# A reordered prologue, rows turned by DMA, and a weight load moved by three steps, in a fused attention and gated-MLP kernel

## The chip, the cores and the metric

One core of a Trainium2 chip. The metric is device time in microseconds (us) of one execution. "Start" below is the time from the beginning of the profile to the first exponential of the attention. A "half" is one head with 1024 of the 2048 queries: 16 steps of one key block each. The half-rate state of TensorE is read below from the distance between the starts of consecutive matmuls: 0.216 us for 512 columns and 0.056 us for 128 at full rate, 0.427 and 0.107 us at half rate (the "cold array" of some passages).

## The reference

A block with adaptive layer norm. Shapes: x is 2048 x 1024, 32 heads of 128 with cached keys and values of 2048 rows, an MLP of 2 x 1792 columns, everything bf16.

```python
mod = (_silu(c) @ w_mod).reshape(c.shape[0], 6, 1, -1)        # sa, ca, ga, sb, cb, gb
h = _layernorm(x, axis=-1) * (1 + ca) + sa
x = x + ga * _A_ref(h, A_k_cache, A_v_cache, A_wq, A_wo)       # q = h @ wq, softmax(q k / sqrt(128)) v, @ wo
h = _layernorm(x, axis=-1) * (1 + cb) + sb
x = x + gb * _B_ref(h, B_w_in, B_w_sp, B_b_sp, B_w_out)        # gelu, layer norm, spatial gate, projection
```

## The kernel before

It runs in stages: a prologue (norm of the first eight row tiles, modulation of h1T, first query product), attention over 64 halves, the output projection with the second norm, then the MLP. Three places matter.

The prologue alternates row loads and modulation-weight loads, and takes head 0's keys through a transposing DMA:

```python
    load_wm(nc.scalar, 0, 1)
    load_wm(nc.scalar, 1, 1)
    for j in range(4):
        for t in range(2):
            nc.sync.dma_start(xg[j][:, t], x_dram[:, 2 * j + t, :])
        load_wm(nc.sync, j, 0)
    ...
    load_wq(0)
    load_kv(0)          # keys with transpose=True
    load_wq(1)
    for fn in q_work(0, 0, bank_ps):
        fn()
    emit_s(0)
    emit_s(1)
```

In attention the loads for the next head, and every fourth head a 1 MB load of query weights, are issued at step 2 of a half. The softmax sums of the half before go through DRAM and a transposing DMA, issued at step 3 in the same queue; VectorE reduces them at step 10:

```python
        if kb == 2 and i < 16:
            load_kv(halves[i + 1][0])
            if i == 12:
                load_wq(2)
        elif kb == 2 and qh == 0 and h + 1 < H:
            load_kv(h + 1)
            if h % 4 == 2 and h + 2 < H:
                load_wq((h + 2) // 4)
        ...
                    {0: store_sums, 3: turn_sums, 10: finish_den, 13: load_rec}).get(kb)
```

In the output projection, each of 16 row tiles is turned into columns on TensorE, one tile behind:

```python
    def to_columns(h, hT, ti):
        hps = bank_ps("hps", [P, KD, P], BF16)
        for dc in range(KD):
            nc.tensor.transpose(hps[:, dc, :], h[:, dc * P:(dc + 1) * P], identity[:])
        nc.vector.tensor_copy(out=hT[:, :, ti * P:(ti + 1) * P], in_=hps[:, :, :])
    ...
    for ti in range(NT):
        ...
        attend_out(ti, range(H) if ti else [H - 1])          # 64 matmuls of 512 columns
        if ti > 0:
            to_columns(hbs.pop(ti - 1), h2T, ti - 1)
```

The softmax here doesn't subtract the row's maximum and nothing guards it: scores larger than these inputs give would overflow.

Of the kernel before, what the change touches and what calls it, by code (L numbers as in the profile page):

```python
# [16 lines left out]
def kernel(  # L17
# [62 lines left out]
    h1_dram = dram.tile([2, P, D], BF16)  # L80
    mod_dram = dram.tile([4, D], FP32)
    rec_dram = dram.tile([2 * H, 1024], FP32)

# [17 lines left out]
    for j in range(4):  # L101
        xg.append(early.tile([P, 2, D], BF16, name=f"xg{j}"))
        wms.append(early.tile([P, 2, KD, 256], BF16, name=f"wm{j}"))

    def load_wm(eng, j, k):
        eng.dma_start(wms[j][:, k], wmod_v[:, :, k * D + j * 256:k * D + (j + 1) * 256])

    load_wm(nc.scalar, 0, 1)
    load_wm(nc.scalar, 1, 1)
    for j in range(4):  # L110
        for t in range(2):
            nc.sync.dma_start(xg[j][:, t], x_dram[:, 2 * j + t, :])
        load_wm(nc.sync, j, 0)

# [24 lines left out]

    def to_columns(h, hT, ti):  # L140
        hps = bank_ps("hps", [P, KD, P], BF16)
        for dc in range(KD):
            nc.tensor.transpose(hps[:, dc, :], h[:, dc * P:(dc + 1) * P], identity[:])  # L143
        nc.vector.tensor_copy(out=hT[:, :, ti * P:(ti + 1) * P], in_=hps[:, :, :])  # L144

    h1T = ring.tile([P, KD, S], BF16, name="h1T")
# [7 lines left out]
    def silu():  # L154
        nc.tensor.transpose(cT_ps[:], c_sb[:, :], identity[:KD, :KD])
        nc.scalar.activation(e_sb[:], cT_ps[:], ACT.Exp, scale=-1.0)
        load_wm(nc.scalar, 2, 1)
        load_wm(nc.scalar, 3, 1)

# [8 lines left out]
    def keep_busy(n):  # L168
        zps = bank_ps("zps", [P, 512])
        for _ in range(n):  # L170
            nc.tensor.matmul(zps[:], zeros[:, 0:P], zeros[:], start=True, stop=True)
# [3 lines left out]
    def mod_products(j):  # L175
        mps = mpss[j] = side_ps("mps", [P, 2, 2])
        for k in range(2):
            for f in range(2):
                for kc in range(KD):
                    nc.tensor.matmul(mps[:, k, f:f + 1], wms[j][:, k, kc, f * P:(f + 1) * P],  # L180
                                     scT[:, kc:kc + 1], start=(kc == 0), stop=(kc == KD - 1))
# [6 lines left out]

    def modulate(dc, t0, eng=nc.vector):
        sl = h1T[:, dc, t0:t0 + 1024]  # L190
        if eng is nc.scalar:
            nc.scalar.activation(sl, sl, ACT.Identity, bias=cols[:, 0, dc:dc + 1],
                                 scale=cols[:, 1, dc:dc + 1])
            return
        nc.vector.tensor_scalar(out=sl, in0=sl, scalar1=cols[:, 1, dc:dc + 1],
                                scalar2=cols[:, 0, dc:dc + 1], op0=ALU.mult, op1=ALU.add)

    row = {}
    silu()
    for ti in range(9):  # L200
        if ti < 8:
            row[ti] = row_stats(xg[ti // 2][:, ti % 2, :])
        if ti == 0:
            silu_end()
        else:
            xt = xg[(ti - 1) // 2][:, (ti - 1) % 2, :]
            centre(xt, row.pop(ti - 1), xt)
            if ti % 2 == 0:
                j = ti // 2 - 1
                hps = wide_ps("hps", [P, 2, KD, P], BF16)  # L210
                for t in range(2):
                    for dc in range(KD):
                        nc.tensor.transpose(hps[:, t, dc, :],
                                            xg[j][:, t, dc * P:(dc + 1) * P], identity[:])
                nc.scalar.activation(
                    h1T[:, :, j * 256:(j + 1) * 256].rearrange("p d (t k) -> p d t k", t=2),
                    hps[:].rearrange("p t d k -> p d t k"), ACT.Copy)
                if j > 0:
                    mod_products(j - 1)
                keep_busy(6)  # L220
            elif ti > 3:
                mod_columns(ti // 2 - 2)
    mod_products(3)
    mod_columns(2)
    for j in range(4):
        if j == 3:
            mod_columns(3)
        modulate(2 * j, 0)
        modulate(2 * j + 1, 0, nc.scalar if j else nc.vector)
    keep_busy(8)  # L230

    wq_v = A_wq.rearrange("(dc p) hd -> p dc hd", p=P)
    wo_v = A_wo.rearrange("(h p) n -> p h n", p=P)
    wq_g = {}
    kts, vs, qts = {}, {}, {}

# [50 lines left out]

    load_wq(0)
    load_kv(0)
    load_wq(1)  # L290
    for fn in q_work(0, 0, bank_ps):
        fn()
    emit_s(0)
    emit_s(1)
# [57 lines left out]

    accs, slabs, hbs = {}, {}, {}

# [23 lines left out]
    def late_rows(g):  # L378
# [3 lines left out]
        if 4 <= g < 100:  # L382
            if r == 0:
                rows[ti] += row_stats(rows[ti][0][:, :]),
                if ti + 1 < NT:
                    load_row(ti + 1)
            elif r == 2:
                xt, st = rows.pop(ti)
                hb = early.tile([P, D], BF16, name="hb1", tag="hb1", bufs=2)
                centre(xt[:, :], st, hb[:])  # L390
                nc.sync.dma_start(h1_dram[ti % 2], hb[:])
            elif r == 6:
                nc.sync.dma_start(out=h1T[:, :, ti * P:(ti + 1) * P], in_=h1_dram[ti % 2],
                                  transpose=True)
        elif 100 <= g < 108:
            modulate(g - 100, 1024)

# [7 lines left out]
    def late_mods(i, kb):  # L405
        n0, odd = divmod(i - 17, 2)
        if n0 < 8 and not odd and kb == 2:
            wm_l[n0] = early.tile([P, KD, 512], BF16, name="wm_l", tag="wm_l", bufs=2)
            nc.sync.dma_start(wm_l[n0][:], wmod_v[:, :, (n0 + 4) * 512:(n0 + 5) * 512])
# [15 lines left out]
        elif i == 33 and kb == 8:  # L425
            wide_rows = early.tile([P, 2, D], FP32, name="wide_rows")
            nc.sync.dma_start(ga[:], mod_dram[0].partition_broadcast(P))
# [5 lines left out]
    for g, (i, kb) in enumerate(steps):  # L433
# [13 lines left out]
        if kb == 2 and i < 16:  # L447
            load_kv(halves[i + 1][0])
            if i == 12:
                load_wq(2)  # L450
        elif kb == 2 and qh == 0 and h + 1 < H:
            load_kv(h + 1)
            if h % 4 == 2 and h + 2 < H:
                load_wq((h + 2) // 4)
        if i == len(halves) - 1 and kb == 7:
# [58 lines left out]
    def load_x(ti):  # L514
        xts[ti] = mid.tile([P, D], BF16, name="x_in", tag="x_in", bufs=3)
        nc.sync.dma_start(xts[ti][:], x_dram[:, ti, :])

    load_x(0)
    load_x(1)
# [4 lines left out]
    for ti in range(NT):  # L524
# [8 lines left out]
        if ti > 0:  # L533
            to_columns(hbs.pop(ti - 1), h2T, ti - 1)
        x1 = mid.tile([P, D], BF16, name="x1", tag="x1", bufs=2)
# [7 lines left out]
        ln_mod(x1[:, :], mod2, hb)  # L543
        hbs[ti] = hb
    right.__exit__(None, None, None)
# [5 lines left out]
    for ti in range(NT):  # L551
        zst = small.tile([P, 4, nc.vector.BN_STATS_DIM], FP32, name="zst", tag="zst")
        for k in range(4):
# [6 lines left out]
            nc.vector.bn_stats(out=zst[:, k, :], in_=z2[ti][:, sl])  # L560
            if ti == 2 and k == 0:
                to_columns(hbs.pop(NT - 1), h2T, NT - 1)
        mv, rstd = ln_stats(zst[:, :, :])
# [114 lines left out]
```

## Time and profile before

Median 1877.88 us over 12 runs (1875.40 to 1880.30).

| read from the trace of before | us |
|---|---|
| start (first exponential) | 34.29 |
| start to the first projection matmul | 1124.61 |
| projection, to the first matmul of the next stage | 227.95 |
| next stage (second MLP half) | 97.43 |
| rest | 391.47 |

The page's first part: busy us of each engine, share of the span, instructions.

```profile
span 1875.7 us, 24842 instructions
PE 1847.7 (99%) x9129; PEld 853.1 (45%) x9129; DVE 1271.8 (68%) x2124; ACT 1099.9 (59%) x1155; POOL 32.7 (2%) x55
```

TensorE is the bound, but its 99% says little about what a piece of its work costs. The Trainium skill, "Perfetto Trace Analysis" (Identifying the Most-Contended Engine), warns that the busy share of matmuls is no good measure of how close a kernel is to its peak, because matmuls are pipelined.

The timeline of TensorE in the projection: start, duration of the merged group, line, output and inputs, count.

```profile
1200.60 0.59 PE L372 MATMUL acc<-wo_t,oT_last 128*128 128x512 bf16 x2
1201.03 0.61 PE L143 MATMUL hps<-identity,hb 128*128 128x128 bf16 x8
1201.47 13.54 PE L372 MATMUL acc<-wo_t,ot 128*128 128x512 bf16 x62
1214.86 0.59 PE L372 MATMUL acc<-wo_t,oT_last 128*128 128x512 bf16 x2
```

A row tile takes 1214.86 - 1200.60 = 14.26 us. The eight transposes are shown as 0.61 us long, but the next group starts 1201.47 - 1201.03 = 0.44 us after them: the durations of pipelined groups overlap.

The waits of VectorE in attention (waiting group, releaser: total us, times, longest):

```profile
DVE den L325 <- DMA pT<-sums_dram: 14.1, 7, 2.9
```

One of these waits, in a half that loads query weights, in two timelines of before: first that of the issuing queue (SPq), then that of VectorE:

```profile
534.26 2.06 SPq L244 DMA_TRANSPOSE kT<-in_A_k_cache_dram  x1
536.41 0.53 SPq L246 DMA_DIRECT2D v_sb<-in_A_v_cache_dram  x1
537.00 1.55 SPq L239 DMA_DIRECT2D wq_t<-in_A_wq_dram  x1
538.60 2.97 SPq L318 DMA_TRANSPOSE pT<-sums_dram  x1
```

```profile
544.04 0.09 DVE L323 MEMSET rec<- 128x32 f32 x1
547.04 1.22 DVE L325 TENSOR_REDUCE den<-pT 128x8 f32<-128x1024 bf16 x1 [2.92 <-DMA pT<-sums_dram]
```

The sums are issued behind the weights, and VectorE, which has casts of the next queries behind this reduction, stands for 2.92 us. TensorE then loses 1.71 us at 550 us. Six such TensorE gaps add up to 6.7 us (distances between the starts of consecutive matmuls in the trace, less the 0.22 us that a matmul takes: 0.95, 0.86, 1.71, 0.73, 1.21, 1.26).

The start of before, on ScalarE: the last line is the first exponential.

```profile
26.97 3.50 ACT L192 ACTIVATE h1T<-h1T,cols 128x1024 bf16<-128x1024 bf16 x3
34.29 2.85 ACT L458 ACTIVATE pt<-sps 128x1024 bf16<-128x1024 f32 x3 [3.82 <-PE sps L282]
```

### The profile page before, as it was taken

What the parts mean: (1) busy time and instruction counts of PE and PEld (TensorE: products, weight loads), DVE (VectorE), ACT (ScalarE), POOL (GpSimd) and SP (SyncE); (2) the same over time, 40 slices, a digit from 0 to 9 for tenths busy, and PEclk for the clock granted to TensorE, in tenths of its full rate; (3) what the DMA queues carried; (4) which work ended last, traced back from release to release, by engine and by line L of the source; (5) the groups of instructions that cost most, each with busy time, mean ns of one, the idle gap of its engine ahead of it and who ended that gap; (6) DMA issues with size and microseconds to landing.
All of it is one profiled execution on the core that took longest, in us unless ns stands there. A gap on an engine that the chain in (4) does not pass through costs nothing.

```text
span 1875.7 us, 24842 instructions
## 1 busy us (share of the span) xinstructions
PE 1847.7 (99%) x9129; PEld 853.1 (45%) x9129; DVE 1271.8 (68%) x2124; ACT 1099.9 (59%) x1155; POOL 32.7 (2%) x55
## 2 busy tenths in 40 slices
PE   7999999999999999999999999999999999999999
PEld 4444444444444444444444444444445444444444
DVE  6898888888888888888888887554465400333334
ACT  5888999988988999989989997000013332000000
POOL 1000000000000000000000000000000000000000
PEclk9999999999999999999999999999999999999999
DMA  9575576465565644565466334664123012221102
GB/s 241 119 169 115 130 162 149 122 158 139 126 163 127 151 129 110 131 165 138 126 164 144 105 91 122 182 199 122 45 65 76 12 46 79 51 52 45 45 1 79
DMA packets 387963, 215.30 MB, mean 115 GB/s; under 512 B 289536, under 2 KB 345856, under 8 KB 387840
## 3 DMA queue, kind: packets, MB, share of 16 engines
q1 hardware_dynamic: 383680, 211.62, 44.3%
q10 hardware_dynamic: 4160, 2.10, 0.4%
q8 instruction: 71, 1.16, 0.3%
q14 instruction: 52, 0.43, 0.1%
HBM read 126.36 MB, written 41.44 MB: 89 GB/s over the span
## 4 chain that ended last, share of the span: by engine, by line
PE 90%; DVE 4%; DMA 4%; issue 1%; SPq 1%; ACT 0%; POOL 0%; DVEq 0%; POOLq 0%
PE sps L282 21%; PE ops L469 20%; PE acc L372 12%; PE gps L607 10%; PE qps L262 10%; PE zps L557 5%; PE bo L628 5%; PE zps L591 5%; DMA pT<-sums_dram 3%; DVE pacc L479 2%; DMA xg<-in_A_x_dram 1%; SPq L239 0%; DVE stats L127 0%; DMA wm<-in_w_mod_dram 0%; DVE den L325 0%
## 5 line engine op out<-in xcount | busy, mean ns | idle before, releaser
L458 ACT ACTIVATE pt<-sps 128x1024 bf16<-128x1024 f32 x1024 | 1017.7, 1025 | 110.2 <-PE sps L282 77.6
L479 DVE TENSOR_TENSOR pacc<-pacc,pt 128x1024 bf16<-128x1024 bf16 x896 | 616.6, 688 | 64.1 <-ACT pt L458 4.7
L282 PE MATMUL sps<-qT,kT 128*128 128x512 bf16 x2048 | 610.0, 379 | 7.0 <-DVE qT L266 6.3
L469 PE MATMUL ops<-pt,v_sb 128*128 128x512 bf16 x2048 | 609.4, 379 | 1.5 <-DVE ou L475 1.2
L262 PE MATMUL qps<-h1T,wq_t 128*128 128x512 bf16 x1024 | 344.4, 379 | 1.5 <-DVE rec L337 1.2
L469 PEld LDWEIGHTS <-v_sb 128*128 128x128 bf16 x2048 | 200.1, 98 | 249.2 <-issue 8.5
L282 PEld LDWEIGHTS <-kT 128*128 128x128 bf16 x2048 | 199.0, 98 | 245.4 <-issue 10.1
L372 PE MATMUL acc<-wo_t,ot 128*128 128x512 bf16 x992 | 216.9, 379 | 0.0
L559 ACT ACTIVATE z<-zps 128x448 bf16<-128x448 f32 x64 | 34.8, 543 | 290.3 <-PE zps L557 287.4
L607 PE MATMUL gps<-wsp,z 128*128 128x512 bf16 x896 | 193.9, 379 | 0.0
L610 DVE TENSOR_TENSOR g<-gps,b_bc 128x512 bf16<-128x512 f32 x56 | 38.7, 692 | 221.8 <-PE gps L607 221.8
L262 PEld LDWEIGHTS <-wq_t 128*128 128x128 bf16 x1024 | 100.2, 98 | 120.8
L372 PEld LDWEIGHTS <-ot 128*128 128x128 bf16 x992 | 96.4, 98 | 113.5
L607 PEld LDWEIGHTS <-z 128*128 128x128 bf16 x896 | 87.7, 98 | 105.7
L266 DVE CAST qT<-qps 128x512 bf16<-128x512 f32 x128 | 88.4, 690 | 42.7 <-PE qps L262 42.6
L557 PE MATMUL zps<-z2w,h2T 128*128 128x448 bf16 x512 | 97.3, 352 | 0.0
L628 PE MATMUL bo<-w_out_t,z1T 128*128 128x512 bf16 x448 | 97.2, 379 | 0.0
L591 PE MATMUL zps<-h2T,z1w 128*128 128x512 bf16 x448 | 96.9, 379 | 0.0
L144 DVE COPY h2T<-hps 128x1024 bf16<-128x1024 bf16 x16 | 11.0, 690 | 97.4 <-PE hps L143 97.4
L346 DVE TENSOR_TENSOR oT<-ou,rbc 128x1024 bf16<-128x1024 f32 x62 | 75.6, 1219 | 1.0 <-DMA rbc<-rec_dram 1.0
L325 DVE TENSOR_REDUCE den<-pT 128x8 f32<-128x1024 bf16 x55 | 65.3, 1188 | 14.1 <-DMA pT<-sums_dram 14.1
L557 PEld LDWEIGHTS <-h2T 128*128 128x128 bf16 x512 | 50.0, 98 | 46.5 <-issue 0.2
(72 smaller groups left out, 689.1 us busy)
## 6 DMA issues: line engine op xcount, KB each, us to landing
rbc<-rec_dram SPq DMA_DIRECT2D x64, 512.0 KB
v_sb<-in_A_v_cache_dram SPq DMA_DIRECT2D x40, 512.0 KB
oT_dram<-oT SPq DMA_DIRECT2D x62, 256.0 KB
sums_dram<-pacc SPq DMA_DIRECT2D x55, 256.0 KB
ot<-oT_dram SPq DMA_DIRECT2D x24, 512.0 KB
wq_t<-in_A_wq_dram SPq DMA_DIRECT2D x8, 1024.0 KB
wm_l<-in_w_mod_dram SPq DMA_DIRECT2D x8, 1024.0 KB
wo_t<-in_A_wo_dram SPq DMA_DIRECT2D x8, 1024.0 KB
```

Source lines behind the costliest of these rows:

```text
L262: nc.tensor.matmul(box["ps"][:], wq_t[:, dc, hc:hc + DH], h1T[:, dc, q0:q0 + 512], start=(dc == 0), stop=(dc == KD - 1))
L266: nc.vector.tensor_copy(out=out_t[:, j * 512:(j + 1) * 512], in_=box["ps"][:])
L282: nc.tensor.matmul(sps[:, j * 512:(j + 1) * 512], kts[h][:, kb * P:(kb + 1) * P], qts[(h, qh)][:, j * 512:(j + 1) * 512], start=True, stop ...
L346: nc.vector.tensor_mul(out=oT[:], in0=state[i]["ou"][:], in1=state[i]["rbc"][:])
L372: nc.tensor.matmul(accs[ti][:, sl], lhs, wo_t[:, hh, sl], start=(hh == 0), stop=(hh == H - 1))
L458: nc.scalar.activation(pt[:], s_tiles.pop(g)[:], ACT.Exp, scale=SCALE)
L469: nc.tensor.matmul(o_ps[j][:], vs[h][:, kb, :], pt[:, j * 512:(j + 1) * 512], start=(kb == 0), stop=(kb == NKB - 1))
L479: nc.vector.tensor_add(out=pacc[:], in0=pacc[:], in1=pt[:])
L557: nc.tensor.matmul(zps[:], h2T[:, dc, ti * P:(ti + 1) * P], z2w[:, dc, sl], start=(dc == 0), stop=(dc == KD - 1))
L591: nc.tensor.matmul(zps[:], w[:, dc, :], h2T[:, dc, q * 512:(q + 1) * 512], start=(dc == 0), stop=(dc == KD - 1))
L607: nc.tensor.matmul(gps[:], z2[s][:, f * P:(f + 1) * P], wsps[q][:, s, :], start=(s == 0), stop=(s == NT - 1))
L628: nc.tensor.matmul(bo[:], z1T[:, f, ti * P:(ti + 1) * P], w_out_t[:, f, sl], start=(f == 0), stop=(f == NF - 1))
```

## The change

Its intent is to start attention earlier, and to take work and stalls off TensorE:

1. Prologue: row tiles first; statistics of two tiles on ScalarE; head 0's keys loaded plainly and turned on TensorE; the last turned tile modulated straight out of PSUM by both ScalarE and VectorE; 13 instead of 32 dummy matmuls.
2. The query-weight load moves from step 2 to step 5 of a half.
3. Rows of the output projection are stored to DRAM and come back through a transposing DMA.

```diff
+    h2_dram = dram.tile([4, P, D], BF16)
 ...
-    for j in range(4):
-        for t in range(2):
-            nc.sync.dma_start(xg[j][:, t], x_dram[:, 2 * j + t, :])
-        load_wm(nc.sync, j, 0)
+    for ti in range(8):
+        nc.sync.dma_start(xg[ti // 2][:, ti % 2], x_dram[:, ti, :])
+    load_wm(nc.sync, 0, 0)
+    load_wm(nc.sync, 2, 1)
+    ...                                   # (1, 0), (3, 1), (2, 0), (3, 0)
+    nc.sync.dma_start(wq_g[0][:, :, 0:256], wq_v[:, :, 0:256])
+    nc.sync.dma_start(k0[:], A_k_cache[0, 0].rearrange("(p j) d -> p j d", p=P))
+    nc.sync.dma_start(vs[0][:], A_v_cache[0, 0].rearrange("(p j) d -> p j d", p=P))
+    nc.sync.dma_start(wq_g[0][:, :, 256:512], wq_v[:, :, 256:512])
 ...
+    turn(1)
+    mod_columns(0)
+    mod_products(1)
+    keep_busy(4)
+    ...
+    turn(2)
+    mod_columns(1)
+    mod_products(2)
+    norm(6)
+    norm(7)
+    turn(3, False)
+    keep_busy(5)
+    mod_products(3)
+    mod_columns(2)
+    for dc in range(4):
+        modulate(dc, 0, 768)
+    mod_columns(3)
+    modulate(7, 0, 768, nc.scalar)
+    for dc in (4, 5):
+        modulate(dc, 0, 768)
+        modulate(dc, 768, 256, nc.scalar, turned_x[3][:, dc, :, :])
+    modulate(6, 0, 768)
+    for dc in range(4):
+        modulate(dc, 768, 256, nc.vector, turned_x[3][:, dc, :, :])
+    for dc in (6, 7):
+        modulate(dc, 768, 256, nc.scalar, turned_x[3][:, dc, :, :])
 ...
-            if i == 12:
-                load_wq(2)
         elif kb == 2 and qh == 0 and h + 1 < H:
             load_kv(h + 1)
-            if h % 4 == 2 and h + 2 < H:
-                load_wq((h + 2) // 4)
+        if kb == 5 and i == 12:
+            load_wq(2)
+        elif kb == 5 and i >= 16 and qh == 0 and h % 4 == 2 and h + 2 < H:
+            load_wq((h + 2) // 4)
 ...
+    def turn_rows(ti):
+        nc.sync.dma_start(out=h2T[:, :, ti * P:(ti + 1) * P], in_=h2_dram[ti % 4],
+                          transpose=True)
 ...
-            to_columns(hbs.pop(ti - 1), h2T, ti - 1)
+            turn_rows(ti - 1)
 ...
-        hbs[ti] = hb
+        nc.sync.dma_start(h2_dram[ti % 4], hb[:])
```

More of the change, by code (lines that the diff above doesn't have):

```diff
@@ L102 @@
         xg.append(early.tile([P, 2, D], BF16, name=f"xg{j}"))
-        wms.append(early.tile([P, 2, KD, 256], BF16, name=f"wm{j}"))
+        wms.append(early.tile([P, 2, KD, 256], BF16, name="wm", tag="wm", bufs=4))
     def load_wm(eng, j, k):
         eng.dma_start(wms[j][:, k], wmod_v[:, :, k * D + j * 256:k * D + (j + 1) * 256])
+    k0 = early.tile([P, NKB, DH], BF16, name="k0")
+    wq_v = A_wq.rearrange("(dc p) hd -> p dc hd", p=P)
+    wq_g, kts, vs, qts = {}, {}, {}, {}
+    for g in range(2):
+        wq_g[g] = att.tile([P, KD, 4 * DH], BF16, name="wq_t", tag="wq_t", bufs=2)
+    kts[0] = att.tile([P, S], BF16, name="kT", tag="kT", bufs=2)
+    vs[0] = att.tile([P, NKB, DH], BF16, name="v_sb", tag="v_sb", bufs=2)
+    nc.scalar.activation(small.tile([P, 1], FP32, name="warm_e")[:], eps_tile[:], ACT.Exp)
     load_wm(nc.scalar, 0, 1)
     load_wm(nc.scalar, 1, 1)
-    for j in range(4):
-        for t in range(2):
-            nc.sync.dma_start(xg[j][:, t], x_dram[:, 2 * j + t, :])
-        load_wm(nc.sync, j, 0)
+    for ti in range(8):
+        nc.sync.dma_start(xg[ti // 2][:, ti % 2], x_dram[:, ti, :])
+    load_wm(nc.sync, 0, 0)
+    load_wm(nc.sync, 2, 1)
+    load_wm(nc.sync, 1, 0)
+    load_wm(nc.sync, 3, 1)
+    load_wm(nc.sync, 2, 0)
+    load_wm(nc.sync, 3, 0)
+    nc.sync.dma_start(wq_g[0][:, :, 0:256], wq_v[:, :, 0:256])
+    nc.sync.dma_start(k0[:], A_k_cache[0, 0].rearrange("(p j) d -> p j d", p=P))
+    nc.sync.dma_start(vs[0][:], A_v_cache[0, 0].rearrange("(p j) d -> p j d", p=P))
+    nc.sync.dma_start(wq_g[0][:, :, 256:512], wq_v[:, :, 256:512])
     def ln_stats(chunks):
@@ L138, in ln_mod @@
         nc.vector.tensor_add(out=h[:], in0=h[:], in1=mod[:, 1, :])
-    def to_columns(h, hT, ti):
-        hps = bank_ps("hps", [P, KD, P], BF16)
-        for dc in range(KD):
-            nc.tensor.transpose(hps[:, dc, :], h[:, dc * P:(dc + 1) * P], identity[:])
-        nc.vector.tensor_copy(out=hT[:, :, ti * P:(ti + 1) * P], in_=hps[:, :, :])
     h1T = ring.tile([P, KD, S], BF16, name="h1T")
@@ L156, in silu @@
         nc.scalar.activation(e_sb[:], cT_ps[:], ACT.Exp, scale=-1.0)
-        load_wm(nc.scalar, 2, 1)
-        load_wm(nc.scalar, 3, 1)
     def silu_end():
@@ L168, in keep_busy @@
     def keep_busy(n):
-        zps = bank_ps("zps", [P, 512])
+        zps = side_ps("zps", [P, 512])
         for _ in range(n):
@@ L175, in mod_products @@
     def mod_products(j):
-        mps = mpss[j] = side_ps("mps", [P, 2, 2])
+        mps = mpss[j] = bank_ps("mps", [P, 2, 2])
         for k in range(2):
@@ L187, in mod_columns, with modulate @@
                                     scalar1=1.0)
-    def modulate(dc, t0, eng=nc.vector):
-        sl = h1T[:, dc, t0:t0 + 1024]
+    def modulate(dc, t0, n, eng=nc.vector, src=None):
+        dst = h1T[:, dc, t0:t0 + n]
+        if src is None:
+            src = dst
+        else:
+            dst = dst.rearrange("p (t k) -> p t k", k=P)
         if eng is nc.scalar:
-            nc.scalar.activation(sl, sl, ACT.Identity, bias=cols[:, 0, dc:dc + 1],
+            nc.scalar.activation(dst, src, ACT.Identity, bias=cols[:, 0, dc:dc + 1],
@@ L193, in modulate @@
                                  scale=cols[:, 1, dc:dc + 1])
             return
-        nc.vector.tensor_scalar(out=sl, in0=sl, scalar1=cols[:, 1, dc:dc + 1],
+        nc.vector.tensor_scalar(out=dst, in0=src, scalar1=cols[:, 1, dc:dc + 1],
                                 scalar2=cols[:, 0, dc:dc + 1], op0=ALU.mult, op1=ALU.add)
-    row = {}
-    silu()
-    for ti in range(9):
-        if ti < 8:
-            row[ti] = row_stats(xg[ti // 2][:, ti % 2, :])
-        if ti == 0:
-            silu_end()
-        else:
-            xt = xg[(ti - 1) // 2][:, (ti - 1) % 2, :]
-            centre(xt, row.pop(ti - 1), xt)
-            if ti % 2 == 0:
-                j = ti // 2 - 1
-                hps = wide_ps("hps", [P, 2, KD, P], BF16)
-                for t in range(2):
-                    for dc in range(KD):
-                        nc.tensor.transpose(hps[:, t, dc, :],
-                                            xg[j][:, t, dc * P:(dc + 1) * P], identity[:])
-                nc.scalar.activation(
-                    h1T[:, :, j * 256:(j + 1) * 256].rearrange("p d (t k) -> p d t k", t=2),
-                    hps[:].rearrange("p t d k -> p d t k"), ACT.Copy)
-                if j > 0:
-                    mod_products(j - 1)
-                keep_busy(6)
-            elif ti > 3:
-                mod_columns(ti // 2 - 2)
@@ new lines, with stats_act, norm @@
+    row, junk = {}, early.tile([P, D], BF16, name="junk")
+    def stats_act(ti):
+        mv = early.tile([P, 2], FP32, name=f"mv{ti}")
+        src = xg[ti // 2][:, ti % 2, :]
+        nc.scalar.activation(junk[:], src, ACT.Identity, scale=1.0 / D, accum_out=mv[:, 0:1])
+        nc.scalar.activation(junk[:], src, ACT.Square, scale=D ** -0.5, accum_out=mv[:, 1:2])
+        row[ti] = (mv, None)
+    def norm(ti):
+        mv, rstd = row.pop(ti)
+        x_t = xg[ti // 2][:, ti % 2, :]
+        centre(x_t, (mv, rstd), x_t)
@@ new lines, in finish_act @@
+    def finish_act(ti):
+        mv = row[ti][0]
+        var = small.tile([P, 1], FP32, name="var", tag="var")
+        nc.vector.scalar_tensor_tensor(out=var[:], in0=mv[:, 0:1], scalar=mv[:, 0:1],
+                                       in1=mv[:, 1:2], op0=ALU.mult, op1=ALU.subtract)
+        nc.vector.tensor_scalar(out=var[:], in0=var[:], scalar1=-1.0, scalar2=EPS,
+                                op0=ALU.mult, op1=ALU.add)
+        rstd = small.tile([P, 1], FP32, name="rstd", tag="rstd")
+        nc.gpsimd.tensor_tensor(out=rstd[:], in0=var[:], in1=neg_half[:], op=ALU.pow)
+        row[ti] = (mv, rstd)
@@ new lines, with turn, dve @@
+    turned_x = {}
+    def turn(j, evacuate=True):
+        hps = turned_x[j] = wide_ps("hps", [P, KD, 2, P], BF16)
+        for t in range(2):
+            for dc in range(KD):
+                nc.tensor.transpose(hps[:, dc, t, :],
+                                    xg[j][:, t, dc * P:(dc + 1) * P], identity[:])
+        if evacuate:
+            nc.scalar.activation(
+                h1T[:, :, j * 256:(j + 1) * 256],
+                hps[:].rearrange("p d t k -> p d (t k)"), ACT.Copy)
+    def dve(ti):
+        row[ti] = row_stats(xg[ti // 2][:, ti % 2, :])
@@ new lines, in turn_k, with out @@
+    def turn_k(j, evacuate=True):
+        k_ps = bank_ps("k_ps", [P, 8, DH], BF16)
+        for kb in range(8):
+            nc.tensor.transpose(k_ps[:, kb, :], k0[:, 8 * j + kb, :], identity[:])
+        def out():
+            nc.scalar.activation(kts[0][:, 1024 * j:1024 * (j + 1)],
+                                 k_ps[:].rearrange("p j d -> p (j d)"), ACT.Copy)
+        if evacuate:
+            out()
+        return out
+    silu()
+    dve(0)
+    silu_end()
+    dve(1)
+    norm(0)
+    stats_act(2)
@@ L223 @@
+    dve(3)
+    norm(1)
+    turn(0)
+    keep_busy(4)
+    mod_products(0)
+    finish_act(2)
+    stats_act(5)
+    dve(4)
+    norm(2)
+    norm(3)
+    turn(1)
+    mod_columns(0)
+    mod_products(1)
+    keep_busy(4)
+    dve(6)
+    norm(4)
+    finish_act(5)
+    dve(7)
+    norm(5)
+    turn(2)
[5 more added lines that the diff above has]
+    keep_busy(5)
     mod_products(3)
     mod_columns(2)
-    for j in range(4):
-        if j == 3:
-            mod_columns(3)
-        modulate(2 * j, 0)
-        modulate(2 * j + 1, 0, nc.scalar if j else nc.vector)
@@ L230 @@
-    keep_busy(8)
-    wq_v = A_wq.rearrange("(dc p) hd -> p dc hd", p=P)
+    for dc in range(4):
[10 more added lines that the diff above has]
+        modulate(dc, 768, 256, nc.scalar, turned_x[3][:, dc, :, :])
@@ L233 @@
     wo_v = A_wo.rearrange("(h p) n -> p h n", p=P)
-    wq_g = {}
-    kts, vs, qts = {}, {}, {}
     def load_wq(g):
@@ L286, in emit_s @@
         s_tiles[g] = sps
-    load_wq(0)
-    load_kv(0)
-    load_wq(1)
-    for fn in q_work(0, 0, bank_ps):
-        fn()
+    nc.sync.dma_start(wq_g[1][:], wq_v[:, :, 512:1024])
+    first = q_work(0, 0, bank_ps)
+    for fn in first[:KD]:
+        fn()
+    turn_k(0)
+    for fn in first[KD:]:
+        fn()
+    turn_k(1)
     emit_s(0)
@@ L351, in normalise @@
         del state[i]
-    accs, slabs, hbs = {}, {}, {}
+    accs, slabs = {}, {}
     def load_slab(s, pl):
@@ L395, in late_rows @@
         elif 100 <= g < 108:
-            modulate(g - 100, 1024)
+            modulate(g - 100, 1024, 1024)
     def load_row(ti):
@@ L407, in late_mods @@
         if n0 < 8 and not odd and kb == 2:
-            wm_l[n0] = early.tile([P, KD, 512], BF16, name="wm_l", tag="wm_l", bufs=2)
+            wm_l[n0] = early.tile([P, KD, 512], BF16, name="wm_l", tag="wm", bufs=4)
             nc.sync.dma_start(wm_l[n0][:], wmod_v[:, :, (n0 + 4) * 512:(n0 + 5) * 512])
@@ L425, in late_mods @@
         elif i == 33 and kb == 8:
-            wide_rows = early.tile([P, 2, D], FP32, name="wide_rows")
+            wide_rows = early.tile([P, 2, D], FP32, name="wide_rows", tag="wm", bufs=4)
             nc.sync.dma_start(ga[:], mod_dram[0].partition_broadcast(P))
@@ L543 @@
         ln_mod(x1[:, :], mod2, hb)
-        hbs[ti] = hb
+        nc.sync.dma_start(h2_dram[ti % 4], hb[:])
+    turn_rows(NT - 1)
     right.__exit__(None, None, None)
@@ L560 @@
             nc.vector.bn_stats(out=zst[:, k, :], in_=z2[ti][:, sl])
-            if ti == 2 and k == 0:
-                to_columns(hbs.pop(NT - 1), h2T, NT - 1)
         mv, rstd = ln_stats(zst[:, :, :])
```

## The prediction

> **What bounds the kernel now.** TensorE. The page's busy table gives PE 99% of a 1875.7 us span, VectorE 68%, ScalarE 59%; clock 1.00. In the timeline most halves of a head (80 matmuls of 512 columns at 0.216 us) take 17.3 us, and a row tile of the output projection 14.26 us: 64 x 0.213 = 13.65 plus 0.61 for eight transposes. So only TensorE work, TensorE stalls and the prologue count. The first exponential starts at 34.29 us.
>
> **The change, part by part.**
>
> 1. Output projection: 128 TensorE transposes and 16 VectorE copies become a store plus a transposing DMA per row tile. Eight transposes occupy TensorE 0.61 us (timeline): 16 x 0.61 = 9.8 us, all critical, since the stage has no TensorE gap. The copies (11.0 us) are off the path. The added traffic (two transfers of 256 KB per 13.65 us) fits: the stage runs at about 150 GB/s (1250 to 1300 us), against 320 in the prologue. The last transpose is needed only at the end of the next stage, some 85 us later. Expected: -9.8 us; tile period 13.65 us.
>
> 2. The 1 MB query-weight load moves from step 2 of a half to step 5, so behind the transposing load of the softmax sums issued at step 3. By the waits, VectorE's denominator reduction waits for that load 14.1 us over 7 times, longest 2.9. Six TensorE gaps of 0.73 to 1.71 us (at 266, 407, 550, 691, 831, 970 us) sit in the six halves that load weights: 6.7 us. Expected: -6 us; those waits almost gone.
>
> 3. Prologue: row tiles are loaded before most modulation weights, two tiles' statistics go to ScalarE, head 0's keys are turned on TensorE instead of by DMA. The DMAs run at 315 to 325 GB/s from 4 to 24 us, so rows plus modulation weights (6.3 MB) cannot land before about 22 us in any order. VectorE needs about 15 us from the first row (estimate: six statistics of 1.55, eight normalisations of 0.54, small ones), so ends about 20 us: DMA limits. Then: last modulation products 0.94 us, modulations to 25-26, first query product (weights land about 24), key transposes, second query product to 28, casts, and a ScalarE key copy of about 1 us just ahead of the first exponential. Estimate: first exponential at 30.0 us, -4.3 us. There are 13 instead of 32 dummy matmuls. The Trainium skill, "TensorE: Matmul & The Clock Gate" (Part 1), says the array starts at half rate and speeds up after about 3.4 us of activity; this trace agrees (dummy matmuls 0.43 us apart until about 16 us, later 0.22). Gaps could cool it again and cost 1-2 us.
>
> The rest of attention, gating and final projection are unchanged; the early halves limited by VectorE (gaps of about 4 us between 70 and 161 us) stay.
>
> **Predicted time.** 1878.2 - 9.8 - 6.0 - 4.3 = 1858 us, 80% range 1853 to 1863. Faster by over 2%: 0.01; within 2%: 0.98; slower by over 2%: 0.01.
>
> **Right if** the first exponential starts at 28.5-31.5 us; the six gaps are gone; the projection period is 13.65 us; later stages are unchanged, less one 0.61 us transpose group. **Wrong if** TensorE waits for projection slabs or transposed rows; new waits for weights or reciprocals appear; matmuls are 0.43 us apart between 20 and 34 us.
>
> **What would make it wrong.** Transposing DMAs slowing the slab loads, which share their queue; a cold array at the start of attention; weights or keys of head 0 landing after 26 us; VectorE debt from the prologue in the early halves.

## The result, and the profile after

Median 1861.10 us over 8 runs (1859.89 to 1862.49). The ratio of the mean of its runs to that of before's runs of the same rounds is 0.9912, 95% interval 0.9902 to 0.9922 (so not quite the ratio of the medians). Executions over 1.5% slower than the fastest of the same kernel are left out of the means. The saving is 1877.88 - 1861.10 = 16.8 us where 19.9 had been predicted: inside the range, within 2%, but with terms that were off in both directions. By stage, from the two traces (one execution each, so their sum, 16.0 us, is not the difference of the medians):

| stage | before | after | change | predicted |
|---|---|---|---|---|
| start | 34.29 | 32.62 | -1.67 | -4.3 |
| start to first projection matmul | 1124.61 | 1117.65 | -6.96 | -6.0 |
| projection | 227.95 | 221.25 | -6.70 | -9.2 |
| next stage | 97.43 | 96.85 | -0.58 | -0.6 |
| rest | 391.47 | 391.35 | -0.12 | 0 |

(The predicted 9.8 is split over two stages, 15 and 1 groups of 0.61.)

The page's first part and TensorE's timeline in the projection, after:

```profile
span 1859.7 us, 24646 instructions
PE 1837.9 (99%) x8998; PEld 845.0 (45%) x8998; DVE 1262.1 (68%) x2110; ACT 1102.8 (59%) x1167; POOL 32.8 (2%) x55
```

```profile
1191.51 0.59 PE L451 MATMUL acc<-wo_t,oT_last 128*128 128x512 bf16 x2
1191.94 13.54 PE L451 MATMUL acc<-wo_t,ot 128*128 128x512 bf16 x62
1205.33 0.59 PE L451 MATMUL acc<-wo_t,oT_last 128*128 128x512 bf16 x2
```

A row tile takes 1205.33 - 1191.51 = 13.82 us, not the predicted 13.65, and TensorE never waits in this stage.

The wait of the reduction for the sums is absent from the list of waits. The queue in a half that loads weights:

```profile
530.29 2.15 SPq L320 DMA_TRANSPOSE kT<-in_A_k_cache_dram  x1
532.54 0.53 SPq L322 DMA_DIRECT2D v_sb<-in_A_v_cache_dram  x1
533.12 2.98 SPq L397 DMA_TRANSPOSE pT<-sums_dram  x1
536.16 0.57 SPq L427 DMA_DIRECT2D oT_dram<-oT  x1
536.77 0.43 SPq L315 DMA_DIRECT2D wq_t<-in_A_wq_dram  x1
```

The sums stand ahead of the weights now. Of the TensorE gaps over 0.3 us between 200 and 1140 us, one of 0.63 us is left, at 635 us; it is none of the six (before has one of 0.50 us at 641 us besides them).

The start in the timelines of after, first on ScalarE, then on VectorE (in brackets: idle before, and what ended it):

```profile
26.40 1.03 ACT L205 ACTIVATE h1T<-h1T,cols 128x768 bf16<-128x768 bf16 x1 [2.00 <-DVE cols L195]
27.33 1.00 ACT L205 ACTIVATE h1T<-hps,cols 128x256 bf16<-128x256 bf16 x2
29.77 1.02 ACT L205 ACTIVATE h1T<-hps,cols 128x256 bf16<-128x256 bf16 x2 [1.44 <-DVE h1T L208]
30.68 2.04 ACT L258 ACTIVATE kT<-k_ps 128x1024 bf16<-128x1024 bf16 x2
32.62 1.02 ACT L537 ACTIVATE pt<-sps 128x1024 bf16<-128x1024 f32 x1
```

```profile
26.22 1.25 DVE L208 TENSOR_SCALAR h1T<-h1T,cols 128x768 bf16<-128x768 bf16 x3
28.36 1.37 DVE L208 TENSOR_SCALAR h1T<-hps,cols 128x256 bf16<-128x256 bf16 x4 [0.89 <-ACT h1T L205]
```

The last modulation columns come at 26.2 us, and then ScalarE, VectorE and ScalarE again read the last turned tile one after another, although four of its eight columns of blocks lie in one PSUM bank and four in the other. The granted TensorE clock in stretches of 4 us (last three columns: clock, DMA share, GB/s) fell below one after TensorE had waited 1.42 us, until 18.12 us, for modulation weights:

```profile
12.00:16.00 4.00, 3.77 (x51) 2.63 (x52) 3.12 (x12) 2.70 (x2) 1.95 (x3) 1.00 1.16 294
16.00:20.00 4.00, 2.58 (x48) 1.76 (x46) 3.83 (x12) 3.12 (x5) 1.25 (x2) 0.86 1.16 290
20.00:24.00 4.00, 4.00 (x66) 3.55 (x65) 1.92 (x8) 1.48 (x1) 0.96 (x1) 0.71 1.17 308
24.00:28.00 4.00, 3.99 (x50) 2.17 (x48) 3.04 (x9) 2.00 (x4) 0.00 (x0) 1.00 1.06 385
```

The clock column needs care here. The trace's clock record begins at 15.5 us and has half rate from 18.9 to 22.3 us; a stretch without a record reads as 1.00, although four dummy matmuls at 13.05 us stand 0.43 us apart. The distances between matmuls tell the state in every stretch.

### The profile page after: what moved, and what is told of

Read it like the earlier page. It is cut to its first block, busy times and chain, and to the rows that moved or that the text cites. A ratio compares the mean times of both kernels' runs of the same rounds, so it can differ in the third digit from the quotient of the medians.

```text
span 1859.7 us, 24646 instructions
## 1 busy us (share of the span) xinstructions
PE 1837.9 (99%) x8998; PEld 845.0 (45%) x8998; DVE 1262.1 (68%) x2110; ACT 1102.8 (59%) x1167; POOL 32.8 (2%) x55
## 4 chain that ended last, share of the span: by engine, by line
PE 94%; DVE 3%; DMA 1%; issue 1%; ACT 1%; SPq 0%; POOL 0%; DVEq 0%; POOLq 0%; ACTq 0%
PE sps L358 22%; PE ops L548 22%; PE acc L451 12%; PE qps L338 11%; PE gps L689 10%; PE zps L641 5%; PE bo L710 5%; PE zps L673 5%; DVE pacc L558 2%; DMA wm<-in_w_mod_dram 0%; DMA xg<-in_A_x_dram 0%; PE mod_ps L494 0%; DVE stats L144 0%; DVE h1T L208 0%; DVE qT L342 0%
## 5 line engine op out<-in xcount | busy, mean ns | idle before, releaser
L622 DVE TENSOR_TENSOR tmp<-acc,ga 128x512 f32<-128x512 f32 x32 | 22.0, 687 | 99.7 <-PE acc L451 99.7
L675 ACT ACTIVATE z1T<-zps 128x512 bf16<-128x512 f32 x56 | 33.4, 597 | 63.3 <-PE zps L673 63.3
```

## The experiments

Twelve kernels, each with five timed rounds and one profile; all gave correct results. Before's median was 1878.24, 1878.27 and 1879.22 us on three chips. The changed kernel was not timed again, so a comparison with it is good to about 1 us, the spread of these medians.

### 1. One part at a time: the rows turned by DMA

Edit: before with part 3 of the diff alone.

> The kernel before with one part of the change alone: rows of the output projection turned by a store and a transposing DMA. Theory A (eight TensorE transposes cost 8 x 0.054 = 0.43 us of pitch, since the profiles show a row tile going from 14.26 to 13.83 us): 7 us faster than before (6.5 to 7.7). Rival B (the prediction's 0.61 us of busy time each): 9.8 us faster, with the missing 2.6 us of the whole change lost elsewhere in it. Rival C (the added DMA traffic costs something): under 6 us, with TensorE gaps in the projection.

Measured: 1869.76 us (1868.30 to 1871.45), ratio 0.9957 (0.9944 to 0.9969). In the profile the projection takes 221.25 us and the next stage 96.86, as in the whole change: 6.70 + 0.57 = 7.3 us off before's. TensorE has no wait for slabs or rows. By the stages theory A holds, and B and C fall. The total alone could not tell them apart: the median difference, 8.5 us, is above A's range, and the interval of the ratio, 0.9944 to 0.9969 or 5.8 to 10.5 us, includes B's 9.8. It also carries the spread of the waits that experiments 3 to 6 are about.

### 2. The suspected cost doubled

```diff
-        for dc in range(KD):
+        for dc in [*range(KD), *range(KD)]:
             nc.tensor.transpose(hps[:, dc, :], h[:, dc * P:(dc + 1) * P], identity[:])
```

> The kernel before with every one of the 128 transposes of the output projection made twice into the same place (the result stays right). Theory A: 16 x 0.43 = 6.9 us slower (6.3 to 7.7), row tile 14.69 us. Rival B (0.61 us for eight): 9.8 us slower, row tile 14.87 us.

Measured: 1884.22 us (1882.88 to 1885.31), ratio 1.0032 (1.0019 to 1.0044), so 6.0 us slower by the medians, a little under the range of A. The stages are sharper than the total: the projection takes 234.65 us, 6.70 more than before, and a row tile 14.71 us in every tile. With 13.81 without transposes and 14.26 with eight, the three kernels put eight transposes at 0.45 us each time. The timeline shows the sixteen:

```profile
1216.95 1.06 PE L143 MATMUL hps<-identity,hb 128*128 128x128 bf16 x16
1218.06 8.15 PE L372 MATMUL acc<-wo_t,ot 128*128 128x512 bf16 x37
```

The Trainium skill, "TensorE: Matmul & The Clock Gate" (Back-to-back issue gap), gives a spacing of columns / 2.4 GHz + 2.5 ns for the isolated case, so 8 x 55.8 ns = 0.45 us as an estimate from that page. This case agrees: 0.45 us.

### 3. One part at a time: the later weight load

Edit: before with part 2 of the diff alone.

> The kernel before with one part alone: the query-weight load at step 5 of a half instead of step 2. Theory: the six TensorE gaps of 0.73 to 1.71 us vanish, 6 to 7 us faster, first exponential unchanged at 34.3 us. Rival (the gaps vanished because of the new prologue's shifted phase): no more than 2 us faster, gaps still there.

Measured: 1871.29 us (1870.71 to 1872.93), ratio 0.9964 (0.9951 to 0.9978). Start to projection took 1118.52 us in its profile, 6.1 less than before; the gaps of the weight loads are gone, and the waits for the sums are down to one:

```profile
DVE den L325 <- DMA pT<-sums_dram: 0.7, 1, 0.7
```

The load alone is worth 6.95 us by the medians. One part of the expectation failed: the start was 35.73 us in this profile, with the same prologue as before's 34.29. In the four profiles with the old prologue it was 34.20, 34.29, 34.79 and 35.73. The trace has the reason: from 23.3 to 26.7 us the clock record shows half rate, and the sixteen transposes that start at 24.52 us stand 0.107 us apart; in the other three profiles the same transposes stand 0.056 us apart.

### 4. The new prologue alone

Edit: the changed kernel with parts 2 and 3 taken back.

> The kernel before with the new prologue alone. Theory (the parts add up): first exponential at 32.6 us as in the whole change, 1.5 to 2.2 us faster than before, and all six gaps of the weight loads still there. Rival (the prologue is worth the predicted 4.3 us but another part of the change takes some back): 3.5 to 5 us faster.

Measured: 1878.76 us (1875.07 to 1881.31), ratio 1.0001 (0.9988 to 1.0014). Neither expectation was met: the start came at 32.95 us, 1.3 us before that of before's profile, yet no time was saved. The trace shows where it went: the waits for the sums were longer than before's,

```profile
DVE den L409 <- DMA pT<-sums_dram: 16.4, 6, 3.6
```

and the six TensorE gaps summed to 9.1 us instead of 6.7. So these waits, which part 2 removes, were 2.3 us longer in this profile, and they blur what this run should have measured.

### 5. The new prologue, with those waits out

Edit: the changed kernel with part 3 alone taken back. It differs from experiment 3 only in the prologue.

> The kernel before with the new prologue and the weight load at step 5, so the changed kernel without the new out-projection turn. The weight load's waits, which differ from run to run, are out of both this kernel and the one with the weight load alone (1871.3 us), so their difference measures the prologue: if it is worth the 1.7 to 2 us that the starts in the profiles show, 1869 to 1870 us. If the prologue is worth nothing, as in the run with the prologue alone, 1871 us; if the predicted 4.3, 1867. Against the changed kernel (1861.1) it should be 7.3 us slower.

Measured: 1868.47 us (1868.08 to 1868.76), ratio 0.9946 (0.9933 to 0.9958): 2.8 us under experiment 3 by the medians, 3.4 by the ratios, with five runs each that do not overlap (the intervals of the two ratios just do). Against the changed kernel it is 7.4 us slower. The prologue is worth about 3 us, more than expected here and less than the 4.3 predicted. The profiles agree once like is compared with like: with TensorE at full rate from 19 us on, the old prologue started attention at 34.20 to 34.79 us and the new one at 31.77 us here and 31.86 us in experiment 6. In this order, load, then prologue, then rows, the steps are 6.95, 2.82 and 7.37 us. That they end at 1861.10 us is no check, since each is the difference of two neighbours in one chain. Taken alone, the parts gave 6.95, -0.5 (experiment 4) and 8.5 us (experiment 1), 14.9 us in all against 16.8 for the whole change, so they did not simply add up.

### 6. Two kernels that differ in the order of two DMA issues

Edit, on the changed kernel: the weight load at step 3, once ahead of the block that issues the transposing load of the sums, once behind it.

```diff
-        if kb == 5 and i == 12:
-            load_wq(2)
-        elif kb == 5 and i >= 16 and qh == 0 and h % 4 == 2 and h + 2 < H:
-            load_wq((h + 2) // 4)
+        if kb == 3 and i == 12:                # "ahead": here; "behind": after work(i - 1)
+            load_wq(2)
+        elif kb == 3 and i >= 16 and qh == 0 and h % 4 == 2 and h + 2 < H:
+            load_wq((h + 2) // 4)
```

> The changed kernel with the query-weight load at step 3 of a half, one place ahead of the transposing load of the softmax sums in the same queue. Theory (queue order: the sums stand behind 1 MB of weights and the reduction at step 10 waits for them): waits of the reduction for the sums come back, 10 us or more over 6 times, 5 to 8 us slower than the changed kernel. Rival (what hurt was the weights colliding with the key and value loads issued at step 2): 0 to 2 us slower.

> The same load at the same step 3, one place behind the transposing load of the sums. Theory (queue order): no such waits (under 1 us), time within 1.5 us of the changed kernel. Rival (time of issue or volume): about the same as with the load one place ahead.

Measured: ahead 1870.13 us (1868.75 to 1872.32), ratio 0.9957 (0.9943 to 0.9970); behind 1861.88 us (1861.43 to 1862.73, 4 runs), ratio 0.9911 (0.9897 to 0.9925). Ahead is 9.0 us slower than the changed kernel, somewhat more than expected; behind is level with it. The waits of the kernel with the load ahead:

```profile
DVE den L404 <- DMA pT<-sums_dram: 14.6, 6, 3.5
```

In the kernel with the load behind, this line does not exist. The queues of the two in the same half, ahead first:

```profile
392.07 1.36 SPq L315 DMA_DIRECT2D wq_t<-in_A_wq_dram  x1
393.49 3.01 SPq L397 DMA_TRANSPOSE pT<-sums_dram  x1
```

```profile
392.27 2.65 SPq L397 DMA_TRANSPOSE pT<-sums_dram  x1
394.97 0.57 SPq L315 DMA_DIRECT2D wq_t<-in_A_wq_dram  x1
```

Same step, same bytes, same neighbours: only the order in the queue differs, so the order is the cause. The Trainium skill, "DMA: Bandwidth & Descriptors" (Queues, rings and completion order), says that each DMA engine takes the descriptors of a ring in order. These two runs agree with it: the sums, 256 KB, stand behind 1 MB.

### 7. TensorE's order in the prologue

TensorE in the changed kernel stood behind modulation weights that came at 18.1 us, cooled, and delivered the last modulation products at 26.0 us. Edit (`turn_half` and `evacuate_x` are `turn` cut into its pieces; their definitions are left out):

```diff
     mod_columns(0)
-    mod_products(1)
-    keep_busy(4)
+    keep_busy(6)
     dve(6)
     norm(4)
     finish_act(5)
+    turn_half(2, 0)
+    mod_products(1)
+    keep_busy(4)
     dve(7)
     norm(5)
-    turn(2)
+    turn_half(2, 1)
+    evacuate_x(2)
     mod_columns(1)
-    mod_products(2)
     norm(6)
     norm(7)
+    mod_products(2)
     turn(3, False)
-    keep_busy(5)
     mod_products(3)
```

> The changed kernel with TensorE's instructions of the prologue in another order, nothing else: dummy matmuls before, not behind, the second modulation products; these between the two halves of the third turn; the third products ahead of the fourth turn; no dummy matmuls ahead of the last products. Theory (TensorE stands in order behind a weight load that lands at 18.1 us, cools, and runs fillers and transposes at half rate, so the last modulation columns come at 26.2 instead of about 24): the last columns at 24.2 to 25.0 us, first exponential 30.8 to 31.6 us, 1.0 to 1.8 us faster than the changed kernel. Rival (the tail behind the last columns, ScalarE and VectorE in turn, sets the start): first exponential within 0.4 us of 32.6.

Measured: 1862.35 us (1861.86 to 1863.96), ratio 0.9918 (0.9906 to 0.9931); start 34.49 us. The first step came true, the last columns were there at 24.8 us (26.3 in the changed kernel). The conclusion did not, and neither did the rival's number: the start became 1.9 us later. The timeline shows why:

```profile
23.45 0.95 PE L189 MATMUL mps<-scT,wm 128*128 128x1 bf16 x32
26.12 3.60 PE L347 MATMUL qps<-h1T,wq_t 128*128 128x512 bf16 x8 [1.72 <-DMA wq_t<-in_A_wq_dram]
```

The query weights landed at 26.1 us whatever TensorE did, and in the 1.72 us of waiting TensorE fell to half rate (by the clock record from 25.21 to 32.04 us): eight matmuls took 3.60 us instead of 1.90, and the granted clock was 0.65 from 24 to 28 us and 0.50 from 28 to 32.

### 8. The changed kernel without its last nine dummy matmuls

Edit: the `keep_busy(4)` behind the second modulation products and the `keep_busy(5)` removed.

> The changed kernel without its last nine dummy matmuls (four behind the second modulation products, five ahead of the last ones). If the fillers are what makes TensorE late: first exponential 0.9 to 1.5 us earlier than 32.6. If the cold array is the cost and the fillers help: transposes and products at half rate up to the attention, first exponential the same or up to 1 us later.

Measured: 1862.22 us (1862.15 to 1862.58, 4 runs), ratio 0.9917 (0.9903 to 0.9930); start 34.17 us. The second case holds, and more strongly than expected (1.55 us later, where up to 1 had been expected): TensorE was at half rate from 18.1 to 31.7 us by the clock record, so already before its first query product waited 0.70 us for weights that landed at 25.8 us and then ran its eight matmuls in 3.60 us. In the changed kernel half rate ended at 22.3 us. The dummy matmuls were not what made TensorE late; they fill a wait for DMA, and without them half rate ended 9.4 us later.

### 9. One PSUM tile of two banks, or two of one bank each

```diff
+    def turn_two(j):
+        parts = [wide_ps("hps", [P, 4, 2, P], BF16),
+                 psum.tile([P, 4, 2, P], BF16, name="hps_b", tag="side", bufs=1)]
+        ...                                # the same 16 transposes
 ...
-    turn(3, False)
     keep_busy(5)
+    turn_two(3)
 ...                                         # readers: turned_x[3][dc // 4][:, dc % 4, :, :]
```

> The changed kernel with the last turned tile in two PSUM tiles of one bank each instead of one tile of two banks (five dummy matmuls move ahead of that turn, to free the second bank). In the changed kernel ScalarE, VectorE and ScalarE again read that tile one after another (waits of 0.9 and 1.4 us). Theory (this alternation is worth about 1.2 us of the start): first exponential 31.2 to 31.7 us, both waits gone. Rival (only the late last columns count): within 0.3 us of 32.6.

Measured: 1860.46 us (1859.30 to 1860.73), ratio 0.9907 (0.9894 to 0.9921); start 31.34 us, as the theory said. The clock record is nearly that of the changed kernel (half rate from 18.6 to 22.0 us), so the two profiles can be compared. From the last modulation columns to the first exponential it takes 5.54 us here and 6.46 us in each of the five profiles with the one tile, so the split is worth 0.92 us of the start; the rest of the 1.28 us is columns that came earlier. (The edit also moves five dummy matmuls, but these lie ahead of the last columns.) Both waits are gone, ScalarE and VectorE read the tile side by side:

```profile
26.04 1.03 ACT L205 ACTIVATE h1T<-h1T,cols 128x768 bf16<-128x768 bf16 x1 [2.00 <-DVE cols L195]
26.97 1.91 ACT L205 ACTIVATE h1T<-hps_b,cols 128x256 bf16<-128x256 bf16 x4
28.77 1.03 ACT L267 ACTIVATE kT<-k_ps 128x1024 bf16<-128x1024 bf16 x1
30.41 1.02 ACT L267 ACTIVATE kT<-k_ps 128x1024 bf16<-128x1024 bf16 x1 [0.61 <-PE k_ps L264]
31.34 1.93 ACT L546 ACTIVATE pt<-sps 128x1024 bf16<-128x1024 f32 x2
```

The Trainium skill, "PSUM — Partial Sum Buffer" (PSUM bank collisions raise a hardware error), says that two engines must not touch the same bank and quadrant at once, two readers included, and that different banks are free. This run agrees with the second half: two engines read two banks together and the result was right. In the changed kernel the readers also read different banks, and yet waited for each other. What differs is the tile: the waits come from the semaphores that the framework puts on a whole tile. As a speed-up the edit is not settled: 1860.46 against 1861.10 us, with overlapping intervals.

### 10. Both edits, and one more step

Edit: experiments 7 and 9 together, and the last 768-column modulation on VectorE.

> The changed kernel with both edits, the TensorE order and the two PSUM tiles, and the last 768-column modulation moved from ScalarE to VectorE. If the two causes add up: first exponential 28.7 to 29.8 us, that is 3 to 4 us earlier than 32.6 and the kernel 3 to 4 us faster than the changed one, about 1857.5 us. If DMA is the floor behind either: the start stays above 30.5 us.

Measured: 1862.25 us (1862.19 to 1863.24, 4 runs), ratio 0.9918 (0.9904 to 0.9931); start 33.23 us. The second case holds: the first query product waited 1.78 us for its weights, until 26.08 us, and TensorE fell to half rate at 27.1 us, in the middle of it.

Then the same with a smaller first weight load and something to do in the wait:

```diff
-    nc.sync.dma_start(wq_g[0][:, :, 0:256], wq_v[:, :, 0:256])
+    nc.sync.dma_start(wq_g[0][:, :, 0:128], wq_v[:, :, 0:128])
 ...                                         # and 128:512 behind the values
     mod_products(3)
+    keep_busy(5, bank_ps)
     mod_columns(2)
```

> The changed kernel with the two PSUM tiles, the TensorE order, the last 768-column modulation on VectorE, and two edits against what held the version with both up (the first query product waited 1.8 us for its weights to land at 26.1 us and then ran at half rate): only head 0's 128 columns of the weights are loaded ahead of the keys (0.26 MB less before them, about 0.9 us), and five dummy matmuls fill the wait. If the landing of the weights is the floor: weights usable at 25.0 to 25.4 us, TensorE at full rate, first exponential 29.8 to 30.8 us, kernel 1858 to 1859.5 us. If the short rows make the load as slow as before, or the array still cools: first exponential 31.3 us or later.

Measured: 1859.87 us (1858.97 to 1861.32, 4 runs), ratio 0.9900 (0.9887 to 0.9914). The profile fell on the slowest of these runs: start 32.46 us. TensorE was at half rate from 24.2 us on, so five dummy matmuls took 2.3 us instead of about 1.1 and held the first query product to 26.41 us:

```profile
24.32 2.29 PE L180 MATMUL zps<-zeros 128*128 128x512 bf16 x5
26.41 2.48 PE L357 MATMUL qps<-h1T,wq_t 128*128 128x512 bf16 x8
```

By the rule set beforehand (start at 31.3 us or later) the second case holds. No wait for weights is listed any more. The semaphore events in the trace show when they landed: the last of sixteen at 25.48 us, against 26.04 us in the kernel before it. So the smaller load came 0.6 us earlier, less than the 0.9 expected, and the dummies at half rate held the first query product back past that gain. This is the lowest median measured, 1.2 us under the changed kernel, with overlapping intervals: not shown to be faster.

## Why the prediction was right, and where it was not

**Total.** 1858 predicted, 1861.1 measured, inside 1853 to 1863 and within 2%. The errors were -2.6 us (rows), -1.5 us (prologue) and +0.9 us (weight load); they add up to -3.2 us, and the time missed by 3.1. Of the prediction's own signs, two held (the six gaps gone; later stages unchanged less one transpose group, 0.58 us) and two failed (the start at 32.62 us, not by 31.5; the row tile at 13.82 us, not 13.65). The total lay in the range because the misses were small against 10 us of range, not because each step held.

**What bounds.** Right. Nothing that VectorE or ScalarE gained counted by itself: the 11 us of VectorE copies that went away show nowhere beside TensorE's 0.45 us per tile.

**1. "Eight transposes occupy TensorE 0.61 us: 16 x 0.61 = 9.8 us."** The mechanism was right, the term was mis-sized. A duration in a timeline of pipelined matmuls includes the tail that overlaps the next group. The distance between starts is what counts: 0.45 us per eight, 16 x 0.45 = 7.2 us, shown by taking them away and by doubling them. The check "64 x 0.213 = 13.65" hid the error, since it was low by what 0.61 was high (13.81 + 0.45 = 14.26). The prediction that the added DMA traffic fits was right: no TensorE wait in the stage.

**2. "The load moves behind the transposing load of the softmax sums."** Right in mechanism, shown by the pair of experiment 6, and slightly low in size: 6.95 us alone (experiment 3), against 6. What the prediction did not see is that these waits seem to differ from run to run. The five kernels with the wait in them spread over 2.4 to 6.2 us in five runs or more, those without it over 0.4 to 2.6 in four runs or more. That the waits cause this spread is likely, not shown.

**3. "First exponential at 30.0 us", by way of "weights land about 24" and "modulations to 25-26".** These steps failed. The last modulation weights, which "cannot land before about 22 us", landed at 23.4 us in the profile after, and TensorE, late behind its half-rate stretch, had their products only at 26.0 us (25.2 us in experiment 5, at full rate). Where TensorE waited for them, the query weights landed at 25.8 to 26.1 us (experiments 5, 7, 8, 10), 2 us later than estimated, and the last modulations ended at 29.7 us on VectorE and 30.8 on ScalarE. The estimate had counted bytes: 6.8 MB had indeed moved by 24.0 us. The packet records of experiment 7 show that from 24 to 26 us keys and values were already moving in 4 KB packets while about 120 of the 512-byte packets that weights consist of were still coming in. The load's sixteen completions came between 24.01 and 26.07 us. So the load lands with its last packets, while bytes of the next loads are already counted; why those packets were late stays open. The second part, readers of one PSUM tile taking turns, is shown by experiment 9: 0.92 us. The prologue is worth about 3 us, not 4.3.

**The cold array.** The prediction named half rate as a risk, at 1-2 us, and it came true. Five profiles have this same prologue, and the distances between matmuls sort them. In two, TensorE was at full rate from 17 us on: starts 31.77 (experiment 5) and 31.86 us (load ahead). In three it was at half rate for some of the time from 17 to 25 us: 32.62 (after), 32.95 (experiment 4) and 33.28 us (load behind). The clock column misleads here, since the last two read 1.00 throughout: their clock records begin only at 24.0 and 24.6 us. The sixteen transposes of the last row tiles show it, first in experiment 5, then with the load behind:

```profile
22.28 1.05 PE L247 MATMUL hps<-identity,xg 128*128 128x128 bf16 x16
```

```profile
23.04 1.80 PE L242 MATMUL hps<-identity,xg 128*128 128x128 bf16 x16
```

In all five, attention starts 6.46 us after the last modulation columns; what half rate moves is when these columns come (25.31 to 26.82 us). So half rate goes with 0.8 to 1.5 us of the start. Why the same prologue falls to half rate, or stays there, in one execution and not in another, no run here shows.

**Open.** Whether the new prologue itself lengthens the waits for the sums when the weight load stands ahead of them (16.4 us in experiment 4, 14.6 with the load ahead in experiment 6, 13.6 to 15.5 with the old prologue in three profiles), or whether that is their spread: one profile of each does not tell.

## What to carry to other kernels

Cost a group of pipelined matmuls by the distance between starts, with and without it, not by its duration or busy time; doubling the group measures it directly. Look at what stands in front of a small, urgent DMA in its queue before looking at bandwidth: moving a 1 MB load behind it was worth 7 us for a change of a few lines. In a prologue that waits for DMA, an engine made ready earlier only waits earlier, and on TensorE the wait can cost more than it saves. Before comparing the starts of two profiles, check by the distance between matmuls that TensorE was at the same rate in both: here that alone was worth up to 1.5 us.

## What the Trainium skill lacked or had wrong

- "TensorE: Matmul & The Clock Gate", Back-to-back issue gap: the page gives about 131 ns per 512-column matmul and 81 ns per 128-column one for real streams of weight loads and matmuls, and calls the formula columns / 2.4 GHz + 2.5 ns the isolated case. In this case's streams the formula holds: 13.81 us / 64 = 216 ns for 512 columns, and 0.45 us / 8 = 56 ns for 128. Part 1 of the same page has these as measured back-to-back values (215.7 and 55.6 ns), so the page disagrees with itself.
- The same page, Part 1: the array is said to go cold after an idle window of about 3.4 us. Here shorter pauses went with half rate: in experiment 7 it began at 25.21 us, 0.81 us after the last product, and no pause in the 3.4 us before that was longer; TensorE had done transposes and one-column products in that time. In experiment 5 a wait of 0.90 us, behind five dummy matmuls of 512 columns and 32 one-column products, left the rate full. The page tells elsewhere of frequent micro-idles that bring half rate, without a length, and that transposes do not count as busy in the same way; whether one-column products count, it does not say.
- "PSUM — Partial Sum Buffer": the page tells of dependencies between engines that touch the same bank and quadrant, but not of waits between readers of different banks of one tile, which the framework orders by tile. It cost 0.9 and 1.4 us of waiting here, 0.92 us of the start.
- "DMA: Bandwidth & Descriptors": the page says that the engines of one load finish independently and that only the full count of 16 means landed, but not how far apart they finish when other loads follow in the queue. Here the sixteen completions of the query weights lay 2.06 us apart (24.01 to 26.07 us, experiment 7), with 6.8 MB moved by 24.0 us; those of the last modulation weights 0.8 us (22.61 to 23.43 us, the profile after).
